# Seven half-size products for the last two down projections, with GpSimd taking sums and butterflies

## Chip, cores, metric

The kernel runs on one core of one Trainium2 chip. The metric is the device time of one execution in microseconds (us). TensorE is called PE in the profile, VectorE DVE, ScalarE ACT, GpSimd POOL and SyncE SP; PEld is PE's weight load.

## The reference

The output is the sum of three terms: the input, a spectral filter of the normalised input (a two-dimensional FFT, a product with complex weights, the inverse), and a gated feed-forward layer of the normalised input.

```python
def reference(A_x, A_w_r, A_w_i, B_x, B_w_gate, B_w_up, B_w_down):
    x = A_x                                    # 1 x 2048 x 512, bf16
    xn = _layernorm(x, axis=-1)
    # A: X = rfft2(xn) * (w_r + 1j w_i);  y = irfft2(X)
    # B: h = gelu(xn @ w_gate) * (xn @ w_up);  h @ w_down     512 -> 1792 -> 512
    return x + _A_ref(xn, A_w_r, A_w_i) + _B_ref(xn, B_w_gate, B_w_up, B_w_down)
```

## The kernel before

The feed-forward layer runs in four chunks of 512 tokens, each of 14 rounds of a gate product and an up product. The FFT's steps are "units" that a list of numbered hooks slips in between those products: D and A forward, B and C the inverse column stage (B reads `tv`, then come a product with the spectral weights `W`, C, and a trip through DRAM scratch), then E and F, which finish the inverse for each of 16 token tiles. F ends in two rounds of butterflies, and its result is added to `x_sb`, where the input and the down projection are summed too. When a tile has both parts, it is stored.

Every operation states what it reads and writes, and a small program works out the semaphore waits from that. An engine's queue therefore runs in exactly the order written here.

```python
        def part_done(j):                       # both parts in: store tile j
            done[j] = done.get(j, 0) + 1
            if done[j] == 2:
                for b in range(2):
                    dma("sp", ov[b, :, j, :], x_sb[64 * b:64 * b + 64, j, :], r=[("acc", j)], w=[("out", j, b)])

        def unit_F(j):
            ...                                 # four matmuls into bank bk
            op("act", lambda e: e.activation(o2, bank(bk), ACT.Copy), r=[("ps", bk)], w=[ok] + (TVK if j < 2 else []))
            ...
            def fin():                          # two rounds of butterflies, on VectorE
                op("dve", lambda e: e.tensor_tensor(uv[:, 0:256], o2[:, 0:256], o2[:, 256:512], ALU.add), r=[ok], w=[uk + (0,)])
                op("dve", lambda e: e.tensor_tensor(uv[:, 256:512], o2[:, 0:256], o2[:, 256:512], ALU.subtract), r=[ok], w=[uk + (1,)])
                op("dve", lambda e: e.tensor_tensor(pos, u2[:, :, 0, :], u2[:, :, 1, :], ALU.add), r=[uk + (0,), uk + (1,)], w=[yk + (0,)])
                op("dve", lambda e: e.tensor_tensor(neg, u2[:, :, 0, :], u2[:, :, 1, :], ALU.subtract), r=[uk + (0,), uk + (1,)], w=[yk + (1,)])
                add_to(j, ys, [yk + (0,), yk + (1,)])
                part_done(j)
            later.append(fin)

        def up(b, fc, jjs=(0, 1, 2, 3), wait=False):
            ...                                 # four matmuls into bank bu
            def mult():                         # frees two PSUM banks and makes hT
                op("dve", lambda e: e.tensor_tensor(hT[b % 2][:, fc, h0:h0 + n], bank(bu)[:, 0:n], gl[k % 3][:, 0:n], ALU.mult), ...)

        def down(b, jj):
            ...                                 # 14 matmuls of 512 columns: hT (stationary) times wd_sb
            add_to(j, bank(bk), [("ps", bk)])   # x_sb += product, on VectorE
            part_done(j)

        # the hooks: at(h, (unit, args)) runs a unit at hook h
        for s, h0 in enumerate((22, 30, 53, 59, 65, 70, 74, 79)):   # loads of the spectral weights W
            ...
        for g in range(9):
            h = int(60 + 4.6 * g)
            if g < 8:
                at(h, (unit_B, g))
            if g > 0:
                at(h, (unit_C, g - 1))
                at(h + 3, (load_vv, g - 1))
        ...
        for j in range(NJ):
            at(113 + 2.2 * j, (unit_E, j))
            at(117 + 2.2 * j, (unit_F, j))
        ...
        for b in range(4):
            for fc in range(NFC):
                gate(b, fc, jjs); hook(False); up(b, fc, jjs); flush(); hook()
                if b > 0 and fc in (2, 5, 8, 11):
                    down(b - 1, (fc - 2) // 3)
        for jj in range(4):
            down(3, jj)                         # the last tile in two halves of 256 columns
```

## Time and profile before

| | before |
|---|---|
| time, median of 3 runs | 188.94 us (188.68 to 189.79) |
| span of the profiled execution | 188.1 us |
| last matmul ends | 183.98 us |
| stall before the first unit B | none (B runs at 76.50 us, `tv` landed at 74.47) |
| VectorE busy, 130 to 190 us | 36.8 us |

The head of the page: the span, each engine's busy time with its share of the span, and the TensorE clock that the throttle granted in 40 slices of the span, in tenths. After these comes the chain of work that ended last, by engine.

```profile
span 188.1 us, 3473 instructions
...
PE 179.9 (96%) x1284; PEld 95.4 (51%) x1284; DVE 110.7 (59%) x262; ACT 88.9 (47%) x143; POOL 39.9 (21%) x90
...
PEclk9999999999999999999999999999999999999998
...
PE 73%; DMA 11%; DVE 9%; ACT 2%; issue 2%; SPq 1%; POOL 1%; DVEq 0%; ACTq 0%
```

PE is busy for 96% of the span, nearly always at full clock, and the chain runs through it. Only what shortens PE's queue, or fills one of its gaps, can shorten this kernel.

The same execution by stages. The header names the columns; the first number after the stretch is its length.

```profile
core 0: us, PE busy (x) PEld busy (x) DVE busy (x) ACT busy (x) POOL busy (x), PEclk, DMA share, GB/s
...
71.00:100.00 29.00, 29.00 (x225) 13.49 (x224) 15.47 (x24) 14.73 (x20) 15.10 (x34) 1.00 0.77 159
...
130.00:160.00 30.00, 30.00 (x203) 16.17 (x202) 20.82 (x58) 16.40 (x30) 3.15 (x11) 1.00 0.16 37
160.00:190.00 30.00, 23.98 (x158) 13.37 (x156) 16.02 (x46) 8.41 (x16) 1.40 (x5) 0.94 0.15 36
```

From 130 us on, where units E and F run, VectorE is busy about two thirds of the time and GpSimd is nearly idle. That is the room which the change wants to use.

The timeline of PE around the first unit B (start, duration, engine, line, operands, count):

```profile
69.72 1.67 PE L738 MATMUL ps<-wd,hT 128*128 128x512 bf16 x7
...
75.54 1.03 PE L700 MATMUL ps<-xnT,wu 128*128 128x512 f16 x4
76.50 0.41 PE L570 MATMUL ps<-tv,be 64*64 64x256 f16 x8
76.84 3.19 PE L738 MATMUL ps<-wd,hT 128*128 128x512 bf16 x14
```

L570 is the first unit B. It needs all of `tv`, whose last transfer has landed 2.0 us earlier; PE does not wait.

Groups of VectorE instructions between 130 and 191 us (busy time, mean ns of one):

```profile
L640 DVE TENSOR_TENSOR x_sb<-tv,x_sb 128x512 bf16<-128x512 bf16 x16 | 6.8, 425 | 0.6
L667 DVE TENSOR_TENSOR tv<-tv 128x256 bf16<-128x256 bf16 x16 | 4.9, 308 | 0.6
...
L668 DVE TENSOR_TENSOR tv<-tv 128x256 bf16<-128x256 bf16 x16 | 4.5, 283 | 0.0
```

L667 and L668 are the second round of butterflies, L640 the add of a tile's result. All have two inputs in SBUF.

### The profile page before, as it was taken

The page shows a single profiled execution, that of the slowest core. Times are in us where ns is not written, and L with a number is a line of the kernel's source. Part 1 is how long each engine was busy: PE and PEld are TensorE (multiplying, and loading weights), DVE is VectorE, ACT ScalarE, POOL GpSimd, SP SyncE. Part 2 cuts the span into 40 slices and gives each one's busy share as a digit, 9 for nine tenths or more (in the row PEclk, how much of TensorE's full clock was granted, in tenths as well). Part 3 has the DMA queues.
Part 4 walks back from the last instruction along what each step waited for, and adds up shares of the span by engine and source line. Part 5 has one row for each costly group of instructions (what it writes and reads, how often), then busy time and mean ns, then how long its engine had stood idle before and what let it go on. Part 6 is the DMA issues. An engine that isn't in the chain of part 4 may idle for free.

```text
span 188.1 us, 3473 instructions
## 1 busy us (share of the span) xinstructions
PE 179.9 (96%) x1284; PEld 95.4 (51%) x1284; DVE 110.7 (59%) x262; ACT 88.9 (47%) x143; POOL 39.9 (21%) x90
## 2 busy tenths in 40 slices
PE   7799999999999999999999999799999999999991
PEld 2388554655555444444444444244555555555460
DVE  3586899996542243456554647223259879699520
ACT  1344547685474522366554463413266566654100
POOL 2110253625000015825726010000011111110000
PEclk9999999999999999999999999999999999999998
DMA  4999999879797278548997976464002212211111
GB/s 126 268 249 303 325 251 310 230 112 211 127 151 128 63 142 132 113 123 203 236 134 133 184 121 134 71 119 93 3 0 56 56 45 70 58 35 26 28 42 42
DMA packets 24977, 24.71 MB, mean 131 GB/s; under 512 B 2832, under 2 KB 22800, under 8 KB 24704
## 3 DMA queue, kind: packets, MB, share of 16 engines
q1 hardware_dynamic: 20992, 18.24, 46.5%
q0 software_dynamic: 1968, 5.14, 11.3%
q10 hardware_dynamic: 2000, 1.11, 2.2%
q8 instruction: 10, 0.16, 0.4%
q14 instruction: 7, 0.06, 0.2%
HBM read 18.19 MB, written 6.29 MB: 130 GB/s over the span
## 4 chain that ended last, share of the span: by engine, by line
PE 73%; DMA 11%; DVE 9%; ACT 2%; issue 2%; SPq 1%; POOL 1%; DVEq 0%; ACTq 0%
PE ps L738 21%; PE ps L700 20%; PE ps L685 20%; DMA scr<-early 8%; DVE st L380 3%; PE ps L649 2%; PE ps L619 2%; DVE hT L706 1%; DMA x_sb<-in_A_x_dram 1%; PE ps L402 1%; DMA out_dram<-x_sb 1%; ACT early L600 1%; DVE cmx L392 1%; POOL rstd L388 1%; PE ps L595 1%
## 5 line engine op out<-in xcount | busy, mean ns | idle before, releaser
L706 DVE TENSOR_TENSOR hT<-ps,gl 128x512 bf16<-128x512 f32 (+1 forms) x62 | 39.1, 637 | 35.3 <-PE ps L700 25.9
L700 PE MATMUL ps<-xnT,wu 128*128 128x512 f16 (+1 forms) x248 | 58.6, 359 | 1.2 <-ACT early L600 1.2
L685 PE MATMUL ps<-xnT,wg 128*128 128x512 f16 (+1 forms) x248 | 58.6, 359 | 0.6 <-ACT xnT L841 0.6
L688 ACT ACTIVATE gl<-ps 128x512 bf16<-128x512 f32 (+1 forms) x62 | 34.3, 556 | 42.6 <-PE ps L685 41.3
L738 PE MATMUL ps<-wd,hT 128*128 128x512 bf16 x210 | 49.1, 379 | 0.0
L685 PEld LDWEIGHTS ps<-xnT,wg 128*128 128x128 bf16 x248 | 23.4, 98 | 21.7 <-issue 1.9
L700 PEld LDWEIGHTS ps<-xnT,wu 128*128 128x128 bf16 x248 | 23.3, 98 | 21.5 <-ACT early L600 1.7
L738 PEld LDWEIGHTS ps<-wd,hT 128*128 128x128 bf16 x210 | 19.7, 98 | 21.9 <-issue 1.0
L640 DVE TENSOR_TENSOR x_sb<-ps,x_sb 128x512 bf16<-128x512 f32 (+1 forms) x17 | 11.2, 660 | 20.9 <-PE ps L738 17.5
L337 POOL DMA_DIRECT2D W<-in_A_w_r_dram x32 | 18.6, 612 | 12.5 <-PE ps L685 8.1
L628 POOL COPY tv<-tv 1x128 bf16<-1x128 bf16 x16 | 4.5, 284 | 53.5 <-ACT tv L626 53.5
L581 DVE TENSOR_TENSOR early<-early,W 128x1024 bf16<-128x1024 f16 x16 | 10.3, 688 | 6.8 <-ACT early L576 6.8
L655 ACT ACTIVATE tv<-ps 128x512 bf16<-128x512 f32 x16 | 9.5, 595 | 9.8 <-PE ps L649 9.8
L447 ACT ACTIVATE early<-ps 128x512 f16<-128x512 f32 x16 | 9.5, 595 | 5.4 <-PE ps L443 5.4
L380 DVE BATCH_NORM_STATS2 st<-x_sb 128x6 f32<-128x512 bf16 x16 | 10.6, 682 | 2.4 <-DMA x_sb<-in_A_x_dram 2.4
L576 ACT ACTIVATE early<-ps 128x1024 f16<-128x1024 f32 x8 | 8.2, 1022 | 6.0 <-PE ps L570 6.0
L626 ACT ACTIVATE tv<-ps 128x512 bf16<-128x512 f32 x16 | 9.6, 598 | 3.0 <-PE ps L619 3.0
L600 ACT ACTIVATE early<-ps 128x1024 bf16<-128x1024 f32 x8 | 8.2, 1022 | 5.8 <-DMA scr<-early 5.8
L479 ACT ACTIVATE early<-ps 128x1024 f16<-128x1024 f32 x8 | 7.9, 1021 | 4.6 <-PE ps L474 3.8
L388 POOL TENSOR_TENSOR rstd<-vpe,mhalf 128x4 f32<-128x4 f32 (+1 forms) x5 | 4.5, 901 | 22.5 <-DVE vpe L387 22.5
L392 DVE TENSOR_SCALAR cmx<-x_sb,ag,rstd 128x512 f16<-128x512 bf16 x16 | 6.2, 421 | 2.1 <-POOL rstd L388 2.1
L559 POOL COPY w<-W 128x4 bf16<-128x4 bf16 x16 | 4.3, 299 | 14.2 <-DMA W<-in_A_w_i_dram 14.2
(75 smaller groups left out, 148.1 us busy)
## 6 DMA issues: line engine op xcount, KB each, us to landing
W<-in_A_w_r_dram POOLq DMA_DIRECT2D x32, 64.2 KB, 3.7
W<-in_A_w_i_dram SPq DMA_DIRECT2D x32, 64.2 KB, 4.5
tv<-scr SPq DMA_DIRECT2D x8, 256.0 KB, 5.2
scr<-early SPq DMA_DIRECT2D x8, 256.0 KB, 4.1
arena<-scr SPq DMA_DIRECT2D x8, 256.0 KB, 4.2
out_dram<-x_sb SPq DMA_DIRECT2D x30, 64.0 KB, 2.0
scr<-early SPq DMA_DIRECT2D x14, 128.0 KB, 3.7
x_sb<-in_A_x_dram SPq DMA_DIRECT2D x6, 256.0 KB, 10.6
```

Source lines behind the costliest of these rows:

```text
L337: op(eng, lambda e: e.dma_start(dst, src), w=list(keys) + list(also), dma=True, after=[("pe", pr.cnt["pe"])])
L380: op("dve", lambda e: e.bn_stats(st[:, j, :], x_sb[:, j, :]), r=[("x", j, 0), ("x", j, 1)], w=[("st", j)])
L447: op("act", lambda e: e.activation(x4.rearrange("p (a c r) -> p a c r", a=2, r=4), bank(bk).rearrange("p (a r c) -> p a c r", a=2, r=4), A ...
L581: op("dve", lambda e, k=k: e.tensor_tensor(pp[i][k], xc[i], W[k][g % 4][:, :, :, 0:256], ALU.mult), r=[("xc", i)] + [key for c in range(2) ...
L600: op("act", lambda e: e.activation(vp[i].rearrange("p c hh k -> p (c hh k)"), pair(bk), ACT.Copy), r=[("ps", bk), ("ps", bk + 1)], w=[("vp ...
L626: op("act", lambda e: e.activation(z, bank(bk).rearrange("p (a c) -> p a c", a=4), ACT.Copy, scale=SC_E), r=[("ps", bk)], w=[zk] + (TVK if ...
L640: op("dve", lambda e: e.tensor_tensor(x_sb[:, j, cs], src, x_sb[:, j, cs], ALU.add), r=r + [("acc", j), ("x", j, 0), ("x", j, 1)], w=[("ac ...
L685: ins = e.matmul(bank(bg)[:, 0:n], wg_sb[:, dc, fc * P:(fc + 1) * P], xnT[:, dc, c0:c0 + n], start=(dc == 0), stop=(dc == 3))
L688: op("act", lambda e: e.activation(gl[k % 3][:, 0:n], bank(bg)[:, 0:n], ACT.Gelu_apprx_tanh), r=[("ps", bg)], w=[("gl", k % 3)])
L700: ins = e.matmul(bank(bu)[:, 0:n], wu_sb[:, dc, fc * P:(fc + 1) * P], xnT[:, dc, c0:c0 + n], start=(dc == 0), stop=(dc == 3))
L706: op("dve", lambda e: e.tensor_tensor(hT[b % 2][:, fc, h0:h0 + n], bank(bu)[:, 0:n], gl[k % 3][:, 0:n], ALU.mult), r=[("ps", bu), ("gl", k ...
L738: ins = e.matmul(bank(bk), hT[b % 2][:, fc, jj * P:(jj + 1) * P], wd_sb[:, fc, :], start=(fc == 0), stop=(fc == NFC - 1))
```

## The change

A chunk of down projection is a product of 512 tokens x 1792 with 1792 x 512. Split both operands in halves each way, and it takes eight half-size products; a known scheme does it in seven, with eight sums of operands first and seven additions after. The change does so for the last two chunks. A matmul of 512 columns becomes one of 256 and a chunk goes from 56 matmuls of 512 columns to 98 of 256, an eighth fewer columns. The operand sums are kept in fp16. Who does the sums:

- the four sums of `w_down` halves (1792 elements in each of 128 partitions): GpSimd;
- four sums of `hT` halves in each of the two chunks, in pieces of 1024, 512 and 256 elements: three on VectorE, one on GpSimd;
- of the additions after, one of 512 and one of 256 elements for each pair of tiles: GpSimd;
- the first round of butterflies in unit F moves from VectorE to GpSimd.

For the operand sums to find their places in memory free, units B, C, E and F and the loads of the spectral weights move ahead by 6 to 12 hooks.

The core of the diff, with cuts marked:

```diff
-            uv = uvt[j % 2]
+            uv = uvt[j % 4]
...
+            op("pool", lambda e: e.tensor_tensor(uv[:, 0:256], o2[:, 0:256], o2[:, 256:512], ALU.add), r=[ok], w=[uk + (0,)])
+            op("pool", lambda e: e.tensor_tensor(uv[:, 256:512], o2[:, 0:256], o2[:, 256:512], ALU.subtract), r=[ok], w=[uk + (1,)])
             def fin():
-                op("dve", ... uv[:, 0:256] ... ALU.add ...)
-                op("dve", ... uv[:, 256:512] ... ALU.subtract ...)
...
-            later.append(fin)
+            at(hk[0] + 3, (fin,))
...
+        def sums_S(b, f0, f1, ks):              # sums of hT halves
+            ...
+                op("pool" if k == 2 else "dve", lambda e, d=d, a=a, b2=b2, o=o: e.tensor_tensor(d, a, b2, o), ...)
+        def sums_T(k):                          # sums of w_down halves, into the old ring of W
+            ...
+            op("pool", lambda e: e.tensor_tensor(T[k], a, b2, ALU.subtract), ...)
+        def product(b, p, step):                # one of seven products: 7 matmuls of 256 columns
+            ...
+            elif step == 3:
+                op("pool", lambda e: e.tensor_tensor(xu..., x_sb[:, jB, :]..., s1..., ALU.add), ...)
+            ...
+            elif step == 5:
+                op("pool", lambda e: e.tensor_tensor(u2, u2, x_sb[:, jA, 256:512], ALU.add), ...)
+            else:
+                add_to(jA, o, rk + [("u2", p)], 1, u2)
...
-        for s, h0 in enumerate((22, 30, 53, 59, 65, 70, 74, 79)):
+        for s, h0 in enumerate((22, 30, 41, 48, 57, 62, 66, 71)):
...
-            h = int(60 + 4.6 * g)
+            h = int(54 + 4.6 * g)
...
-            at(113 + 2.2 * j, (unit_E, j))
-            at(117 + 2.2 * j, (unit_F, j))
+            at(102 + 2.4 * j, (unit_E, j))
+            at(106 + 2.4 * j, (unit_F, j))
...
-                if b > 0 and fc in (2, 5, 8, 11):
+                if b in (1, 2) and n in (2, 5, 8, 11):
                     down(b - 1, (n - 2) // 3)
+                if b == 3:
+                    for f0, f1 in {7: ((0, 4),), 11: ((4, 6),), 13: ((6, 7),)}.get(n, ()):
+                        sums_S(3, f0, f1, (0, 1, 2, 3))
+                    product(2, n // 7, n % 7)
-        for jj in range(4):
-            down(3, jj)
+        for step in range(7):
+            for p in range(2):
+                product(3, p, step)
```

Some smaller things ride along. The two halves of a tile in the last chunk get keys of their own, so that adding one half no longer waits for the other half's store. Each read-back from the DRAM scratch in the column stage (`load_vv`) is queued one unit later. The rounds of the last two chunks run in another order (0, 7, 1, 8, ...), so that both halves of `hT` are ready together. And the second token tile is normalised earlier at the start.

## The prediction

> **What bounds it.** TensorE. The page has PE busy 179.9 of 188.1 us. By the timeline, little is lost after 33 us but one stall of 1.2 us at 119.5 us (waits: an up matmul behind the ScalarE eviction of the inverse column stage, itself behind a scratch DMA) and the tail: last matmul 183.98 us, end 188.10. The last add starts 1.15 us late, behind the other half's output DMA.
>
> **Matmuls removed.** A 512-column matmul starts every 216 ns, a 256-column one every 109 ns (timeline of the tail). A chunk of down projection goes from 56 x 216 ns = 12.1 us to 98 x 109 ns = 10.7 us; two chunks save 2.8 us, all on the PE path.
>
> **Column-stage stall.** Each scratch read-back is queued one unit later, so the queue no longer stops behind a transfer just issued: I expect the 1.2 us to go.
>
> **New stall at the first inverse unit B.** It moves from hook 60 to 54, that is from 76.5 us to right after a 14-matmul down product that ends at 71.2 us. It needs all of tv, whose last load was issued at 68.35 us and landed at 74.47 us (DMA landings). I expect 2.5 to 3.5 us of idle PE, which gives the saving back.
>
> **Start, tail.** Normalising tile 1 earlier frees about 0.5 us at 8 us, but at 12.3 us PE waits for a weight DMA: about 0. In the tail the false wait goes, but the last six products issue ten output DMAs on SP at 0.5 to 0.6 us, against 0.76 us per product: about 0.
>
> **VectorE and GpSimd.** From 137 to 172 us DVE is busy 28.8 of 35 us (windows). It loses 0.57 us of butterfly per tile, 16 tiles, and gets two rounds of sums of about 4.2 us and about 1.5 us of PSUM adds a chunk: about even. GpSimd takes six sums of 1792 elements and 32 butterflies of 256. The trace has no plain two-input GpSimd operation; the Trainium skill, "GPSIMD Engine Reference", section 3.1, gives 4497 ns for 2048 fp32 elements, so I estimate 0.65 us a butterfly, 3.9 us a 1792-sum, some 55 us of GpSimd work in 57 us. The skill's "SBUF — State Buffer", "Who interferes with whom", says that a GpSimd read and a DVE operation with two SBUF inputs exclude each other; the trace agrees (weight copies of 0.18 us took 0.64 and 0.66 us beside a DVE product of 0.69 us; butterflies of 0.29 us took up to 0.42 us). Per tile that is about 1.3 us GpSimd plus 1.0 us DVE out of 2.45 us, before the operand sums. I expect both to run late in the fourth chunk and cost PE 0 to 6 us.
>
> **Sum.** 188.9 - 2.8 - 1.2 + 3.0 = 187.9; start and tail -0.6; lateness +0.5, with a long upper tail: **187.8 us, range 185.4 to 193.5**. Faster by over 2%: 0.08; within 2%: 0.67; slower: 0.25.
>
> **What would show it.** PE idle before the first B unit, ended by the tv DMA; none at the column stage's eviction; 256-column matmuls from wd or wring at 109 ns; butterflies on GpSimd of 0.6 to 0.7 us, DVE butterflies above 0.29 us; PE gaps in the last 45 us ended by hT products or zt copies.
>
> **What would make it wrong.** tv landing by 72 us (then about 185); a GpSimd sum near 1 ns an element; or full exclusion, with PE held by DVE for 5 us or more (above 192).

## The result and the profile after

| | before | after |
|---|---|---|
| time, median of 4 runs | 189.3 us (188.68 to 189.79) | 211.48 us (210.28 to 213.88, one of them slow) |
| ratio | | 1.1153 (1.1065 to 1.124) |
| span of the profiled execution | 188.1 us | 208.0 us |
| TensorE idle within it | 8.2 us | 26.0 us |
| VectorE busy | 110.7 us | 140.8 us |
| GpSimd busy | 39.9 us | 92.4 us |

The result is correct and 11.5% slower. Here and below a ratio is the mean time of one kernel's fast runs over that of the other's of the same rounds, with a 95% interval, so it is not quite the ratio of the medians that stand beside it.

The head of the page after, in the order of before:

```profile
span 208.0 us, 3669 instructions
...
PE 182.0 (87%) x1346; PEld 103.5 (50%) x1354; DVE 140.8 (68%) x263; ACT 90.7 (44%) x147; POOL 92.4 (44%) x140
...
PEclk9999999999999967999999999999999999995899
...
PE 49%; DVE 29%; DMA 9%; issue 7%; SPq 2%; ACT 1%; POOL 0%; ACTq 0%; DVEq 0%
```

PE does fewer columns but is idle for 13% of the span; in two places its clock is cut; and VectorE, which held 9% of the chain, now holds 29%.

The stages after:

```profile
core 0: us, PE busy (x) PEld busy (x) DVE busy (x) ACT busy (x) POOL busy (x), PEclk, DMA share, GB/s
...
71.00:100.00 29.00, 24.24 (x192) 10.94 (x193) 12.06 (x19) 12.92 (x17) 9.79 (x21) 0.88 0.70 133
...
130.00:160.00 30.00, 25.89 (x200) 15.93 (x198) 29.55 (x44) 17.32 (x31) 24.30 (x36) 1.00 0.11 27
160.00:190.00 30.00, 21.15 (x154) 13.23 (x155) 29.42 (x51) 10.71 (x19) 17.11 (x24) 0.94 0.08 18
```

There are two separate troubles. Between 71 and 100 us PE is idle for 4.8 us, and the mean clock of the stage is 0.88. From 130 us on VectorE is busy for 59.0 of 60 us, with fewer instructions (44 in the first stretch instead of 58), and PE loses time again.

PE around the first unit B, now at L573:

```profile
69.75 2.11 PE L853 MATMUL ps<-wd,hT 128*128 128x512 bf16 x9
76.51 0.64 PE L573 MATMUL ps<-tv,be 64*64 64x256 f16 x8 [4.65 <-DMA tv<-scr]
77.08 1.89 PE L817 MATMUL ps<-xnT,wg 128*128 128x512 f16 x4
```

The unit waits 4.65 us for the transfer into `tv`. After it four matmuls of 512 columns take 1.89 us where they took 1.03: the clock is halved. By the clock records that lasts from 74.0 to 80.9 us.

PE's waits over the whole span (us in total, times, longest):

```profile
PE ps L719 <- DVE x_sb L649: 7.1, 2, 5.1
PE ps L622 <- DVE hT L838: 4.8, 2, 3.0
PE ps L573 <- DMA tv<-scr: 4.7, 1, 4.7
...
PE ps L778 <- issue: 1.0, 1, 1.0
```

L719 is the half-size product, L649 an addition into `x_sb`, L838 the product that makes `hT` and frees PSUM. So apart from the transfer, PE waits above all for VectorE. The last line, a wait of unit F at 133.8 us that the profile gives no cause for, is one for GpSimd itself: unit F reads a row that GpSimd copies, and that copy (133.94 to 134.69 us) stands in GpSimd's queue behind a sum of `w_down` (129.98 to 134.00 us). The VectorE groups that answer to those shown of before, and the operand sums:

```profile
L800 DVE TENSOR_TENSOR tv<-tv 128x256 bf16<-128x256 bf16 x16 | 11.3, 705 | 0.0
L649 DVE TENSOR_TENSOR x_sb<-tv,x_sb 128x512 bf16<-128x512 bf16 x16 | 8.6, 540 | 0.6
L801 DVE TENSOR_TENSOR tv<-tv 128x256 bf16<-128x256 bf16 x16 | 7.8, 486 | 0.0
L685 DVE TENSOR_TENSOR xnT<-xnT,hT 128x1024 f16<-128x1024 f16 x1 | 5.5, 5489 | 0.0
L685 DVE TENSOR_TENSOR early<-early,hT 128x1024 f16<-128x1024 f16 x1 | 4.0, 3950 | 0.0
L685 DVE TENSOR_TENSOR early<-hT 128x1024 f16<-128x1024 bf16 x1 | 3.9, 3883 | 0.0
```

The same butterfly that took 308 ns takes 705, its twin 486 instead of 283, the add of a tile 540 instead of 425. An operand sum of 1024 elements took between 1.15 and 5.49 us. (In a later run with no GpSimd arithmetic the same sums took 0.68 to 0.69 us.) The product L838, which has one input in PSUM, kept its length: 682 ns against 689. What VectorE did in that time, beside GpSimd, from 166 to 172 us. First VectorE:

```profile
166.71 5.49 DVE L685 TENSOR_TENSOR xnT<-xnT,hT 128x1024 f16<-128x1024 f16 x1
172.23 1.92 DVE L685 TENSOR_TENSOR cmx<-hT,xnT 128x1024 f16<-128x1024 bf16 x1
174.07 0.68 DVE L838 TENSOR_TENSOR hT<-ps,gl 128x512 bf16<-128x512 f32 x1
```

And GpSimd:

```profile
166.79 2.12 POOL L685 TENSOR_TENSOR xnT<-hT 128x1024 f16<-128x1024 bf16 x1
168.87 0.66 POOL L793 TENSOR_TENSOR tv<-tv 128x256 bf16<-128x256 bf16 x1
169.50 0.66 POOL L794 TENSOR_TENSOR tv<-tv 128x256 bf16<-128x256 bf16 x1
170.11 0.28 POOL L631 COPY tv<-tv 1x128 bf16<-1x128 bf16 x1
170.36 0.66 POOL L793 TENSOR_TENSOR tv<-tv 128x256 bf16<-128x256 bf16 x1
170.99 0.66 POOL L794 TENSOR_TENSOR tv<-tv 128x256 bf16<-128x256 bf16 x1
171.60 0.74 POOL L631 COPY tv<-tv 1x128 bf16<-1x128 bf16 x1
```

One VectorE instruction stands for 5.49 us while GpSimd carries out six instructions, a sum and five more, at their ordinary lengths; only the seventh, the copy at 171.60 us, is stretched (0.74 us; 0.28 undisturbed), and in it the VectorE sum ends. The busy share counts this waiting as work. PE's stall of 3.0 us at 171.8 us ends when the product at 174.07 us at last comes through:

```profile
174.80 0.40 PE L622 MATMUL ps<-be,arena 128*128 128x128 f16 x4 [2.97 <-DVE hT L838]
```

To add it up, I took for each stage the time between the starts of matmuls less what their columns need (216 ns for 512 columns, 109 ns for 256). This is my own sum over the trace's records. Eight of the 112 full-width down products are missing from the trace after; they are counted as work where they are missing.

| what | change of PE's time, us |
|---|---|
| fewer columns | -2.9 |
| up to 71 us | +0.5 |
| 71 to 100 us: stall at the first unit B and the half clock after it | +6.7 |
| 115 to 130 us: the old stall behind the column stage's eviction is gone | -1.2 |
| 130 to 190 us: stalls behind VectorE, 1.0 us of it behind GpSimd | +14.0 |
| 190 us on: half clock after the last of these stalls (5.1 us) | +1.8 |
| last matmul to end of span: 5.07 instead of 4.12 us | +0.95 |

The sum is +19.9, as the spans differ. The 0.5 us up to 71 us can be scatter: in experiment 6 ScalarE's instructions at 13 us come 0.9 us later than in the kernel before, ahead of anything that its edit touches.

### The profile page after: what moved, and what is told of

Read it like the earlier page. It is cut to its first block, busy times and chain, and to the rows that moved or that the text cites. A ratio compares the mean times of both kernels' runs of the same rounds, so it can differ in the third digit from the quotient of the medians.

```text
span 208.0 us, 3669 instructions
## 1 busy us (share of the span) xinstructions
PE 182.0 (87%) x1346; PEld 103.5 (50%) x1354; DVE 140.8 (68%) x263; ACT 90.7 (44%) x147; POOL 92.4 (44%) x140
## 4 chain that ended last, share of the span: by engine, by line
PE 49%; DVE 29%; DMA 9%; issue 7%; SPq 2%; ACT 1%; POOL 0%; ACTq 0%; DVEq 0%
PE ps L832 13%; PE ps L817 12%; PE ps L853 8%; PE ps L719 7%; DVE hT L838 6%; DVE early L685 5%; DVE tv L800 4%; DMA wu<-in_B_w_up_dram 4%; DVE xnT L685 4%; DMA tv<-scr 3%; DVE tv L801 3%; DVE x_sb L649 2%; DMA scr<-early 2%; DVE st L383 2%; SPq L337 2%
## 5 line engine op out<-in xcount | busy, mean ns | idle before, releaser
L838 DVE TENSOR_TENSOR hT<-ps,gl 128x512 bf16<-128x512 f32 (+1 forms) x62 | 39.3, 634 | 25.3 <-PE ps L832 21.0
L853 PE MATMUL ps<-wd,hT 128*128 128x512 bf16 x104 | 24.2, 379 | 0.4
L340 POOL DMA_DIRECT2D wring<-in_A_w_r_dram x32 | 18.6, 612 | 12.9 <-PE ps L817 10.4
L853 PEld LDWEIGHTS ps<-wd,hT 128*128 128x128 bf16 x112 | 10.9, 98 | 12.3 <-issue 0.2
L584 DVE TENSOR_TENSOR early<-early,wring 128x1024 bf16<-128x1024 f16 x16 | 10.3, 686 | 7.5 <-ACT early L579 7.5
L649 DVE TENSOR_TENSOR x_sb<-ps,x_sb 128x512 bf16<-128x512 f32 (+1 forms) x12 | 7.2, 599 | 11.8 <-PE ps L853 11.2
L793 POOL TENSOR_TENSOR tv<-tv 128x256 bf16<-128x256 bf16 x16 | 11.0, 685 | 6.9 <-ACT tv L784 6.9
L579 ACT ACTIVATE early<-ps 128x1024 f16<-128x1024 f32 x8 | 8.2, 1020 | 13.1 <-PE ps L573 13.1
L794 POOL TENSOR_TENSOR tv<-tv 128x256 bf16<-128x256 bf16 x16 | 11.5, 719 | 0.0
L800 DVE TENSOR_TENSOR tv<-tv 128x256 bf16<-128x256 bf16 x16 | 11.3, 705 | 0.0
L622 PE MATMUL ps<-be,arena 128*128 128x128 f16 x64 | 6.2, 219 | 4.8 <-DVE hT L838 4.8
L750 POOL TENSOR_TENSOR tw<-x_sb,tw 128x512 f32<-128x512 bf16 x4 | 4.6, 1160 | 12.5 <-DVE tw L748 12.5
```

Of the source, the lines that this page charges most:

```text
L340: op(eng, lambda e: e.dma_start(dst, src), w=list(keys) + list(also), dma=True, after=[("pe", pr.cnt["pe"])])
L649: op("dve", lambda e: e.tensor_tensor(x_sb[:, j, cs], src, x_sb[:, j, cs] if x is None else x, ALU.add), r=r + keys + [("x", j, 0), ("x", ...
L794: op("pool", lambda e: e.tensor_tensor(uv[:, 256:512], o2[:, 0:256], o2[:, 256:512], ALU.subtract), r=[ok], w=[uk + (1,)])
L853: ins = e.matmul(bank(bk), hT[b % 2][:, fc, jj * P:(jj + 1) * P], wd_sb[:, fc, :], start=(fc == 0), stop=(fc == NFC - 1))
```

## The experiments

For the lateness from 130 us on there are two theories. **A**: GpSimd's reading of SBUF shuts out those VectorE instructions that have two inputs in SBUF. The Trainium skill, "SBUF — State Buffer", section "Who interferes with whom", says that a VectorE instruction with two SBUF inputs contends with a GpSimd instruction that reads SBUF, "not with one that only writes it", and that the loser "fully blocks". **B**, the rival: the work comes too late or is too much in itself; the chain from product to butterfly to add has got a slow engine in it, and VectorE has more to do, so PE would wait whether or not the two engines exclude each other. The stall at the first unit B and the tail have experiments of their own. Twelve kernels ran. They ran on three chips, four on each, with shared runs of the kernel before: experiments 1 to 4; 5, 6, 8 and 9; 7, 10, 11 and 12. So I compare across these groups by ratio to the kernel before. "Slow" beside a run says that it took over 1.5% longer than the fastest of the same kernel; the ratios use the other runs, called fast, alone.

### 1. The butterflies back on VectorE

```diff
-            op("pool", ... uv[:, 0:256] ...)       # right after the eviction
-            op("pool", ... uv[:, 256:512] ...)
             def fin():
+                op("dve", ... uv[:, 0:256] ...)
+                op("dve", ... uv[:, 256:512] ...)
```

> The changed kernel with one part undone: the 32 first inverse butterflies are back on VectorE, in the place they had before. Theory A (a GpSimd operation that reads SBUF shuts out every VectorE operation with two SBUF inputs, and a row of GpSimd operations keeps it out until the row ends): most of the 16 us that the changed kernel loses after 130 us goes; the second butterfly on VectorE returns from 0.71 to about 0.29 us; time about 197 to 201 us. Rival B (VectorE simply has too much work in the last chunk, or seven half-size products suit TensorE badly): VectorE now has 9 us more, so no gain or a loss, 210 us or more. The stall before the first unit B and its half clock stay in both, about 7 us.

Measured: 206.95 us (205.58 to 212.36, one slow), ratio 1.0896 (1.0847 to 1.0944). The butterflies' second round fell to 350 and 317 ns, but the two operand sums at 126 us stayed at 3.88 and 3.95 us, for they stand beside the GpSimd sums of `w_down` and not beside butterflies; a stall of 5.4 us behind VectorE remained in the fourth chunk. The expectation was missed: the butterflies alone give back 2.6 points of 11.5. What follows is that they aren't the whole cause, and that VectorE is close to full once it has them again (busy 14.6 of 15 us from 160 us on, such waiting included).

### 2. The inverse column stage later

The column saving and all GpSimd work stay; only units B and the loads before them move back.

```diff
-        for s, h0 in enumerate((22, 30, 41, 48, 57, 62, 66, 71)):
+        for s, h0 in enumerate((22, 30, 48, 54, 60, 64, 68, 72)):
-        for i, h0 in enumerate((46, 56, 65, 74)):
+        for i, h0 in enumerate((52, 60, 66, 74)):
-            h = int(54 + 4.6 * g)
+            h = 58 + 4 * g
```

> The changed kernel with only the inverse stage's first units later: unit B from hook 58 on every 4 hooks (was 54, every 4.6), and the loads of the filter and of the column matrices that must follow it or that ran ahead of the tv load moved back. Theory: the 4.8 us of idle TensorE before the first unit B goes, the 7 us of half clock that followed it goes with it, so 71 to 100 us loses 1 to 2 us instead of 8; time about 203 to 205 us, with the stalls after 130 us unchanged. Rival (TensorE would wait anyway later, as the column stage and its read-back are what limits): same time, the idle moved to the first unit E.

Measured: 204.53 us (203.41 to 206.28), ratio 1.08 (1.0725 to 1.0876). The wait for `tv` is 0.5 us and the clock stays whole there; the later stalls stand as they were (5.1 us behind `x_sb`, 3.0 behind `hT`). As expected: the two troubles are independent, and this one is worth 3.5 points, or 6.7 us of 189.3.

### 3. No arithmetic on GpSimd, and B late

Experiments 1 and 2 together, and all the sums that GpSimd had go to VectorE.

```diff
-                op("pool" if k == 2 else "dve", lambda e, d=d, ...
+                op("dve", lambda e, d=d, ...
-            op("pool", lambda e: e.tensor_tensor(T[k], ...
+            op("dve", lambda e: e.tensor_tensor(T[k], ...
-                op("pool", lambda e: e.tensor_tensor(xu...      # and the same for u2
+                op("dve", lambda e: e.tensor_tensor(xu...
```

> Both of the above, and every other two-input sum that the change gave GpSimd (the four of wd, one of each operand round, the partial-result sums) on VectorE too; the seven products and fp16 sums stay. Theory A: no shut-out is left, all VectorE sums run at 0.3 to 0.7 us; if VectorE keeps up, the 2.8 us of the fewer columns and the 1.2 us of the old column-stage stall are gained: 185 to 187 us. But by its durations VectorE has about 59 us of work in the last 58 us of hooks, so I expect a few us of TensorE waiting for it: 187 to 192 us. Rival B (products or sheer VectorE load): 200 us or more.

Measured: 191.66 us (190.28 to 192.81), ratio 1.011 (1.0039 to 1.018). Giving VectorE more to do made the kernel 13 us faster than experiment 2. VectorE groups of this run between 130 and 191 us:

```profile
L649 DVE TENSOR_TENSOR x_sb<-tv,x_sb 128x512 bf16<-128x512 bf16 x16 | 6.8, 425 | 0.6
...
L800 DVE TENSOR_TENSOR tv<-tv 128x256 bf16<-128x256 bf16 x16 | 4.8, 299 | 0.6
L801 DVE TENSOR_TENSOR tv<-tv 128x256 bf16<-128x256 bf16 x16 | 4.7, 295 | 0.0
...
L685 DVE TENSOR_TENSOR xnT<-xnT,hT 128x1024 f16<-128x1024 f16 x1 | 0.7, 692 | 0.0
```

Every group has its undisturbed length again; the sum that stood for 5.49 us takes 0.69. From this run the price of the help can be worked out. At VectorE's speed, what GpSimd had taken over is 20.8 us (butterflies 9.1, `w_down` sums 4.4, `hT` sums 2.8, the additions after 4.5). VectorE is busy 130.6 us here, so it had 109.8 us of work of its own in the changed kernel, yet was busy 140.8 us: taking 20.8 us off it cost it 31 us of waiting. What is left over is in part a share of theory B: VectorE is busy 40.9 of the 44 us from 128 to 172 us, one stall of 2.9 us behind it remains, and the clock is halved for 3.4 us after it. But of the 2.9 us by which the span is still longer than before, 1.6 lie in the tail (5.68 instead of 4.12 us after the last matmul), which experiments 8 and 10 are about.

### 4. GpSimd as busy, but without reading

The two butterflies of each tile on GpSimd are replaced by writes of a constant, with as much time spent. The result is wrong (relative error 0.028).

```diff
-            op("pool", lambda e: e.tensor_tensor(uv[:, 0:256], o2[:, 0:256], o2[:, 256:512], ALU.add), r=[ok], w=[uk + (0,)])
-            op("pool", lambda e: e.tensor_tensor(uv[:, 256:512], o2[:, 0:256], o2[:, 256:512], ALU.subtract), r=[ok], w=[uk + (1,)])
+            op("pool", lambda e: e.memset(dumm[:], 0.0), r=["dumm"], w=["dumm"])
+            op("pool", lambda e: e.memset(uv[:, 0:256], 0.0), r=[ok], w=[uk + (0,)])
+            op("pool", lambda e: e.memset(dumm[:], 0.0), r=["dumm"], w=["dumm"])
+            op("pool", lambda e: e.memset(uv[:, 256:512], 0.0), r=[ok], w=[uk + (1,)])
```

> Wrong result on purpose. The changed kernel with each GpSimd butterfly replaced by two GpSimd fills (512 and 256 elements), which read no SBUF but keep the engine busy for about as long and keep every semaphore order. Theory A (reads shut VectorE out): VectorE's second butterflies and its x additions return to about 0.29 and 0.43 us and most of the loss after 130 us goes, as in the kernel with the butterflies back on VectorE: 196 to 202 us. Rival C (GpSimd is only late, and VectorE waits for its results by semaphore, whatever it does with the port): 208 us or more.

Measured: 201.08 us (200.14 to 205.94, one slow), ratio 1.061 (1.0547 to 1.0674). The VectorE groups of this run:

```profile
L649 DVE TENSOR_TENSOR x_sb<-tv,x_sb 128x512 bf16<-128x512 bf16 x16 | 7.6, 477 | 0.6
L803 DVE TENSOR_TENSOR tv<-tv 128x256 bf16<-128x256 bf16 x16 | 6.3, 394 | 0.0
L802 DVE TENSOR_TENSOR tv<-tv 128x256 bf16<-128x256 bf16 x16 | 5.0, 311 | 0.0
```

GpSimd was as busy as in the changed kernel (94.1 us against 92.4), but VectorE's butterflies went from 705 and 486 ns to 311 and 394. VectorE's inputs did come a little sooner, on average 1.4 us after the eviction instead of 2.0, since the first fill does not wait for it; but that isn't what helped, for in all 16 tiles of both kernels VectorE comes to its butterflies later than that, on average 4.0 us after its inputs are ready in the changed kernel and 2.0 here. So it is the reads that matter. They are worth 5.4 of the 11.5 points. This is the run that separates A from B: A holds for the lengths. What remains above the undisturbed lengths I put down to GpSimd's remaining sums; no run separates that.

### 5. The butterflies on GpSimd, in the kernel before

The one part of the change that was to relieve VectorE, put alone into the kernel before, with four buffers for it and the second round three hooks later, as in the changed kernel.

```diff
+            op("pool", ... uv[:, 0:256] ...)
+            op("pool", ... uv[:, 256:512] ...)
             def fin():
-                op("dve", ... uv[:, 0:256] ...)
-                op("dve", ... uv[:, 256:512] ...)
...
-            later.append(fin)
+            at(hk[0] + 3, (fin,))
```

> The kernel before with one part of the change alone: the 32 first inverse butterflies on GpSimd (four buffers, the rest three hooks later). Theory A: VectorE's second butterflies grow from 0.29 to 0.4 us or more and its x additions from 0.43 to above 0.5, the 9 us taken off VectorE are largely given back, but without operand sums both just keep up: 188.5 to 192 us. Rival (the butterflies are the whole cause): 198 us or more. If offloading simply works: 189 us with shorter VectorE busy time, by 9 us.

Measured: 190.35 us (188.75 to 191.62), ratio 1.0007 (0.9938 to 1.0076). In its profile (that execution was slow, at a clock of 0.998, so I read only VectorE's and GpSimd's lengths from it) the second round took 360 and 448 ns instead of 308 and 283, the add of a tile 621 instead of 425. VectorE was rid of 9.2 us of butterflies and its busy time fell from 110.7 to 109.3 us, while GpSimd's rose by 23.7. The relief is nearly all given back, and does no harm only because VectorE has slack there.

### 6. Unit B early, in the kernel before

```diff
-        for s, h0 in enumerate((22, 30, 53, 59, 65, 70, 74, 79)):
+        for s, h0 in enumerate((22, 30, 41, 48, 57, 62, 66, 71)):
-        for i, h0 in enumerate((52, 62, 71, 80)):
+        for i, h0 in enumerate((46, 56, 65, 74)):
-            h = int(60 + 4.6 * g)
+            h = int(54 + 4.6 * g)
...                                             # and the read-backs of the scratch, as in the change
```

> The kernel before with the other part alone: the changed kernel's hooks for the filter loads, column matrices, units B and C and the read-back. Theory: 4.8 us of idle TensorE at the first unit B, ended by the tv load, then 3.4 to 6.8 us of half clock costing 2 to 3 us, minus the 1.2 us of the old column-stage stall: 194 to 196.5 us. Rival (TensorE would catch up the idle later): 189 to 191 us.

Measured: 196.26 us (196.16 to 196.94), ratio 1.0355 (1.0307 to 1.0402). PE's longest wait in it:

```profile
PE ps L570 <- DMA tv<-scr: 5.0, 1, 5.0
```

After it the clock is halved from 75.7 to 82.5 us, and the stall at the column stage's eviction is gone. So the new order alone reproduces the first trouble, at the same 3.5 points which experiment 2 took away.

### 7. Unit B early, the loads where they were

The stall was longer than I had worked out because `tv` itself came later (landed at 76.27 instead of 74.47 us), after its predecessor in the scratch (69.91 instead of 67.93). About 0.5 us of that is a later execution as a whole; from the issue of the last write to the scratch to the landing of `tv` it is 11.3 us instead of 10.0. The suspects are the loads of spectral weights, moved ahead of those transfers.

```diff
-        for s, h0 in enumerate((22, 30, 41, 48, 57, 62, 66, 71)):
+        for s, h0 in enumerate((22, 30, 53, 56, 59, 63, 67, 72)):
-        for i, h0 in enumerate((46, 56, 65, 74)):
+        for i, h0 in enumerate((55, 58, 65, 74)):
```

> The kernel before with units B and C at the changed kernel's hooks, but the filter and column-matrix loads that the change moved ahead of the last tv load kept behind it. Theory: tv lands at about 74.5 us as in the kernel before and not at 76.3, so TensorE idles 3.0 to 3.4 us at the first unit B instead of 5.2; with a shorter idle the half clock may not come: 190.5 to 193.5 us, against 196.3 with the loads early. Rival (the loads have nothing to do with it): 196 us.

Measured: 194.97 us (194.09 and 195.85), ratio 1.0273 (1.0187 to 1.0359). The stall is 3.9 us instead of 5.2 by matmul starts, and the half clock after it 3.4 us instead of 6.8. The expectation was missed on the slow side: the loads account for about 1.3 us of the stall (from the last write's issue to the landing 10.4 us, against 11.7 in experiment 6; one execution each) and half of the time at half clock, but a stall of 3.9 us is still enough for a half clock. This execution also had a half clock from 8.6 to 12.0 us, which had nothing to do with the edit; from there on to the stall its times are 0.8 us later than experiment 6's.

### 8. Seven products in the last chunk alone

From experiment 3, since VectorE is too full for two rounds of operand sums beside units E and F:

```diff
-        for k in range(4):
-            at(..., (sums_S, 2, ...))
-                if b in (1, 2) and n in (2, 5, 8, 11):
+                if b > 0 and n in (2, 5, 8, 11):
-                    product(2, n // 7, n % 7)
```

> The kernel without GpSimd sums and with the later unit B, with the seven products for the last chunk alone (the third is done in eight again). Theory: in that kernel TensorE lost about 4.7 us after 160 us because VectorE, never excluded but full from 140 to 172 us, was behind; without the third chunk's operand sums and half-size additions VectorE has about 9 us less there, so the stall and the half clock go, and 1.4 us of columns are saved: 185.5 to 187.5 us. Rival (seven half-size products cost TensorE something of their own, in weight loads or PSUM turns): 188 us or more, with idle TensorE between the products of the tail.

Measured: 190.56 us (189.53 to 191.42, six runs), ratio 1.0045 (1.0003 to 1.0088). A miss, but not on PE: the last matmul ends at 182.95 us, a microsecond before that of the kernel before. The time goes in the tail, 5.67 us instead of 4.12. SyncE issues 14 stores of half tiles from 176.6 us on, mostly 0.64 us apart and up to 0.89 in the end, with the last at 186.18 us, more than 3 us after the last matmul.

### 9. The control: eight products, all else as in 8

```diff
-        for step in range(7):                   # and no operand sums
-            for p in range(2):
-                product(3, p, step)
+        for jj in range(4):
+            down(3, jj)
```

> The control for it: the same kernel with eight products everywhere, no operand sums, but the new order of the read-back loads, the split of the x key in the tail and the later unit B. Theory: the 1.2 us stall at the column stage and the 1.1 us of false wait in the tail go, nothing else: 186.5 to 188 us, and 1 to 1.6 us slower than the one with seven products for the last chunk. Rival: the two are equal, or this one is faster.

Measured: 188.71 us (188.42 to 189.46, six runs), ratio 0.9953 (0.9911 to 0.9995). This keeps the read-back order, the separate keys of the half tiles and the moved units, and its stores are whole tiles again but for the last. PE ends at 183.97 us as before, and the tail is 3.02 us instead of 4.12. So by the profiles the half per cent is that of the tail, where the false wait has gone, and the seven products must be judged against this control.

### 10. The stores of the tail on two queues

From experiment 8:

```diff
-                    for bb, eng in ((0, "sp"), (1, "act" if step == 6 else "sp")):
+                    for bb, eng in ((0, "sp"), (1, "act")):
```

> The kernel with seven products in the last chunk alone, with one edit: in the tail the output DMA of the second half of the tokens goes out on ScalarE's queue for every product, not only for the last two. Theory: SP's queue, at 0.64 us an issue without pause, is what ends that kernel 5.7 us after its last matmul; with half of its issues gone the end follows the last matmul by about 3.0 to 3.4 us as in the control with eight products, so the time falls by 2.2 to 2.7 us, to 187 to 188.5 us. Rival (the transfers, not their issue, are slow, or TensorE sets the end): no change.

Measured: 187.61 us (187.29 to 189.54, six runs), ratio 0.9911 (0.9856 to 0.9967); the tail is 3.05 us. As expected: SyncE's queue was the limit of the tail.

### 11. The tail tuned

From experiment 10: the second and third step change places, so that the first product that needs an operand sum comes later, and one tile of each pair is stored whole.

```diff
-        for step in range(7):
+        for step in (0, 2, 1, 3, 4, 5, 6):
...
-                out_half(jB, 0)
...
-                out_half(jB, 1)
+                for bb, eng in ((0, "sp"), (1, "act")):
+                    dma(eng, ov[bb, :, jB, :], x_sb[64 * bb:64 * bb + 64, jB, :], r=acc(jB), ...)
```

> The same, and two more edits of the tail: the third product runs before the second, which waits for VectorE's last operand sum (0.8 us of idle TensorE in the profile), and the second tile of each pair is sent whole after its second half. Theory: the idle time goes, another 0.5 to 1 us: 186.2 to 187.8 us, faster than the kernel before by 1 to 1.6% and than the control with eight products by about 1 us. If it only ties with the control, seven products are not worth their sums here even in one chunk.

Measured: 187.63 us (186.57 to 189.43, six runs, one slow), ratio 0.9875 (0.9826 to 0.9923). It cannot be told from experiment 10 (the intervals overlap widely), though the 0.8 us gap behind the operand sums is gone from its trace. It is the best version: 1.2% faster than the kernel before. Against the control, which ran on another chip, it is 0.8 points, and those intervals overlap a little, so the gain of the seven products themselves is likely, with PE ending 1.3 us earlier in the profiles, but not settled by these runs.

### 12. The sums of `w_down` in pieces

If a long GpSimd instruction is what keeps VectorE out, short ones should let it in between. From the changed kernel:

```diff
-            op("pool", lambda e: e.tensor_tensor(T[k], a, b2, ALU.subtract), ...)
+            for f in range(7):
+                op("pool", lambda e, f=f: e.tensor_tensor(T[k][:, f, :], a[:, f, :], b2[:, f, :], ALU.subtract), ...)
```

> The changed kernel with each of the four 1792-element sums on GpSimd cut into seven pieces of 256 elements, in a row without waits. If GpSimd and VectorE take turns instruction by instruction, a VectorE operand sum that took 3.9 us beside them waits for one piece at most and takes 1.5 us or less. If a row of queued GpSimd operations keeps VectorE out until the row ends, it still takes 3 us or more. The whole time moves little in either case, 206 to 213 us.

Measured: 213.69 us (213.05 and 214.33), ratio 1.1259 (1.117 to 1.1348), no better. But the lengths changed: the three operand sums from 126.5 us on took 2.06 (mostly beside a GpSimd sum of 2.12 us that was not cut), 1.04 and 1.04 us, and GpSimd's pieces up to 1.1 us instead of 0.66 in that stretch.

```profile
128.59 1.04 DVE L685 TENSOR_TENSOR early<-early,hT 128x1024 f16<-128x1024 f16 x1
```

There the two engines took turns, instruction by instruction. So it isn't so that a row of GpSimd instructions keeps VectorE out until the row ends. Yet in the same run the case of 5.49 us came again, at the same place in the program:

```profile
169.88 5.48 DVE L685 TENSOR_TENSOR xnT<-xnT,hT 128x1024 f16<-128x1024 f16 x1
```

GpSimd again carried out a sum and five more instructions at ordinary lengths meanwhile. It came in experiment 2 too (5.48 us); in experiment 4, with fills for butterflies, the same sum took 2.75 us. What decides who is next, I did not find out.

That the kernel got no faster has another reason, which the trace shows: PE stood still for 5.45 us in unit F, waiting for GpSimd's copy of one row, which stood in GpSimd's queue behind the last of the pieces (to 138.76 us). In the changed kernel this wait was 1.0 us.

```profile
138.71 0.28 POOL L631 COPY tv<-tv 1x128 bf16<-1x128 bf16 x1
...
139.09 0.58 PE L781 MATMUL ps<-gm,tv 128*128 128x128 f16 x4 [5.45 <-issue]
```

## Why the prediction was wrong

Predicted 187.8 us (185.4 to 193.5), measured 211.48. Point by point, in its order:

- **What bounds it, and the columns removed: right.** The columns save 2.9 us of PE.
- **The stall at the column stage's eviction, "I expect the 1.2 us to go": right.** PE loses 1.2 us less there, and experiment 6 shows it from the reordering alone.
- **The new stall at unit B, "2.5 to 3.5 us of idle PE": the mechanism right, the term mis-sized.** It measured 4.8 us of idle and 6.7 in all. Two things were missing. I took the landing of `tv` from the trace of before, though the change moves loads ahead of it; it came 1.8 us later (0.5 us of it a later execution), and experiment 7 gives about 1.3 us of the stall to the loads. And I counted no half clock. The Trainium skill, "TensorE: Matmul & The Clock Gate", Part 1, puts the clock at half after an idle window of about 3.4 us; in this trace 6.8 us ran at half clock around the stall. My own range of idle time came up to that window, and by the traces less is enough: 2.2 us within a step of 3.4 us (last section).
- **Start: right**; PE then waits for a weight transfer, and nothing is gained. **Tail, "about 0": slightly off**, +0.95 us. I had 0.5 to 0.6 us for a store issued on SyncE; one after the other they mostly come 0.64 us apart. Experiments 8 and 10 show this queue to be the limit.
- **GpSimd's own lengths: right.** 0.69 and 0.72 us for a butterfly (predicted 0.65), 3.57 to 3.80 us for a sum of 1792 (predicted 3.9). The Trainium skill, "GPSIMD Engine Reference", section 3.1, was a good base: its 4497 ns for 2048 elements give an estimate of 2.2 ns an element, and about 2.0 was measured here.
- **"I expect both to run late in the fourth chunk and cost PE 0 to 6 us", entered in the sum as +0.5: this is the step that failed.** It cost 14.0 us, and 1.8 us more of half clock. The exclusion itself was named, and "full exclusion, with PE held by DVE for 5 us or more" stood among what would make the prediction wrong, but it was not added up. The prediction wrote VectorE's account as "about even", as if the two engines worked side by side, and left the exclusion to the tail of the range. Experiment 3 shows that having GpSimd do the arithmetic costs the kernel 13 us, although it takes work off VectorE, experiment 4 that for the butterflies it is the reads, and experiment 5 that even in the kernel before the relief is given back.

The numbers for the sum stood in the prediction. If what GpSimd reads and what VectorE reads twice exclude each other, their times add: some 55 us of GpSimd, 16 tiles of 1.0 us on VectorE, and two rounds of sums of 4.2 us make 79 us, in the 57 us which the prediction had for it. That estimate of 22 us too much, worked out afterwards from its own figures, is nearer the measured lateness than the 0.5 that it entered. It is an upper one, since not all of it need fall on PE.

Theory B has a share, but a smaller one: with all arithmetic on VectorE the kernel is still 1.1% slower than before, in part because VectorE is full where both rounds of sums fall beside units E and F, in part because of the stores in the tail. With seven products in one chunk only, the stall is gone.

What stays open: why one VectorE sum was passed over by six GpSimd instructions in three runs, while in another stretch the engines took turns; and whether the seven products by themselves are worth their 0.8 points.

## What to carry to other kernels

Two engines that exclude each other are one resource: add up the times of the instructions that exclude each other, and compare the sum with the stage, before calling work "moved" from one to the other. A busy engine can be a waiting one; compare the mean length of the same instruction before and after, not the busy share. When a change moves a consumer earlier, work out anew when its data lands if loads move too, and when TensorE could be idle for over 2 us within 3.4 us, count a half clock after it. Ask too what else stands in the queue of the engine that helps: a long sum delays a short copy behind it.

## What the Trainium skill lacked or had wrong

- "SBUF — State Buffer", "Who interferes with whom", has the exclusion right: GpSimd instructions that read nothing, no shorter in total, let VectorE's butterflies go from 705 to 311 ns. It says that who starts first has the ports for the whole instruction, but not who is next when both queues are full. Here one sum on VectorE was passed over by six GpSimd instructions (5.49 us, and 5.48 in two other runs), although by the trace it started before the first of the six (166.71 against 166.79 us), and elsewhere the engines took turns (1.04 us a sum).
- The same page gives no sum for planning. Here 20.8 us of VectorE work given to GpSimd cost VectorE 31 us of waiting.
- "TensorE: Matmul & The Clock Gate", Part 1, gives an idle window of about 3.4 us, free-running, but not how much idle makes a window idle. In all 14 traces the clock changes in steps of 3.41 us. After the first 10 us and up to the last matmul, each step at full clock with 2.18 us or more of idle PE (by the matmul records) was followed by one at half clock (13 steps), and none with 1.88 us or less was. This is why the stall of 2.9 us in experiment 3 (2.28 us of it in one step) was followed by 3.4 us of half clock, and that of 3.0 us in the changed kernel (1.18 and 1.78 us in two steps) was not. Two steps of half clock (6.8 us) followed the stall of 4.8 us.
- "GPSIMD Engine Reference", section 3.1, has 2048 fp32 elements alone for a two-input sum; for 16-bit operands this case shows 2.0 ns an element (1792 elements, 3.57 us undisturbed), and 0.66 us for 256.
- "DMA: Bandwidth & Descriptors" has a latency of the first byte for a transfer issued by SyncE, but for how fast that queue issues it has only 512 sequencer cycles a copy, for "previous generations", in its comparison with a later chip. Here stores on one queue are mostly issued 0.64 us apart, which set the end of the kernel in experiment 8.
